# A fused attention and gated FFN on one Trainium2 core: an attention window of 128 + 104 keys, transposes and PV placed one step later from step 20, and the last output tile in two halves

## The chip, the core and the metric

The kernel runs on one core of one Trainium2 chip. The metric is the device time of one execution, in microseconds. Of before there are three timed runs and one profiled execution.

## The reference

Two stages, all in float32. First an attention with a narrow mask; its output, heads side by side, is then the input of a gated FFN with a convolution over the sequence.

```python
B, H, S, D = 4, 8, 768, 64            # d_model 512, d_ff 1024
n_global, n_local = 8, 96
scores = q @ k.T / sqrt(D)
rel = pos[:, None] - pos[None, :]
keep = (pos[None, :] < n_global) | ((rel >= 0) & (rel < n_local))
dist = where(is_global & ~is_local, n_local, abs(rel))
scores = where(keep, scores - slope[h] * dist, -1e9)
a = exp(scores - max); a = a / (sum(a) + 1e-9)
x = a @ v                              # heads side by side: (B, S, 512)

h = maximum(x @ w_in, 0)
c = conv_w[0]*h[t-1] + conv_w[1]*h[t] + conv_w[2]*h[t+1]
out = (h * sigmoid(c)) @ w_out
```

## The kernel before

**Attention steps.** A sequence has two halves (`u` = 0, 1) of 384 positions (`TB`), a half has three blocks of 128 queries, and heads go in four pairs. A *job* `m` is one batch, one half and one head pair: 32 jobs, in the order batch, half, pair, so that four jobs with `u` = 0 alternate with four with `u` = 1. A *step* `s` is one block of a job: 96 steps, three to a job. A block of queries sees 232 keys (`WIN`): the 96 before it, its own 128, and the 8 global ones. These lie in two chunks: the 128 keys from 96 before the block up to its 32nd own key, then the 8 global keys with the other 96 own keys (104). The first block of a sequence (`first`: `u` = 0, block 0) has no keys before it: it works on 136 keys, of which 32 lie in the first chunk and 104 in the second. There are 16 such blocks, one in each job with `u` = 0.

A step is: `scores` (TensorE matmuls per head: one in plain float32 in the first nine jobs, L359; later two in float32r, L369), `maxima` (VectorE adds the bias table and takes the minimum, L386), `exps` (ScalarE, into one of three buffers `pbuf`, L398), `normalise` (reciprocal on VectorE, L410; the scaling on GpSimd, L416, and up to step 39 for the second head on ScalarE, L414), `transposes` (four on TensorE, L424 and L425, to PSUM, and a copy to `pt` by ScalarE, L431, or in two parts for a first block, L428 and L429). When the three blocks of a job are there, `values` does PV: for each block and chunk one float32 matmul per head, the two heads side by side in the array's columns (L447). In the trace a plain float32 PV matmul is two records. `mixed` then splits the result into two float32r parts, `xh` and `xl` (L459, L460).

**FFN.** For each half `n`: eight groups `h` of 12 matmuls of 384 columns (L478, `relu` into `hbuf` L488), the convolution (L524 GpSimd, L525 and L526 VectorE), tanh (L544), a test that its values are not saturated (`sat`, L555), the gate and its split (L577 to L580), and output tiles `o` of 128 rows by 512 columns, 24 matmuls each (L589), copied (L603) and stored. Its matmuls are the fill: they are put in portions between the attention work of the steps (`fill`).

**What sets the order.** Up to step 10 (`HAND` = 11) the order on every engine is that of the code. After that a scheduler places what the loop hands it; the loop issues in step `s` the scores, maxima and exps of `s`, the normalisation of `s` − 1, the transposes of `s` − 2 (`LAG_T`) and, where a job ends there, the PV of step `s` − 4 (`LAG_V`). The fill is spread by `e = s - LAG_V - 1`: the FFN of a half joins the queue when its last job has been mixed. SyncE issues nearly all loads in one queue, among them `v` (L113, two buffers, so the load of a job waits for the PV of the job before the last), `rk` (L104) and `rq` (L105), which GpSimd casts (L125, L131).

**The end.** Each engine's program holds a second, general path (`general`), which runs if the inputs do not suit the fast one. From step 96 on the weights' words are loaded once more and tested in 16 pieces (`check_load` L314, `check_piece` L321 on VectorE and L325 on ScalarE). After the last output tile, whose two column halves ScalarE (L597) and VectorE (L599) copy and two queues store (L600, L601), the matmul `total` (L832) and one comparison (L833) make a flag; every engine reads it (L936) and branches over `general` (L937). L944 is the closing barrier.

## Time and profile before

| | |
|---|---|
| timed runs | 464.76, 466.29, 466.71 us; median 466.29 |
| profiled execution | 466.18 us |
| its span, first to last instruction | 464.2 us |
| TensorE matmul busy | 443.3 us, 96% of the span |
| VectorE, ScalarE, GpSimd busy | 354.5, 304.4, 223.0 us |
| DMA | 60.01 MB, mean 129 GB/s |

The profiled execution takes 2.0 us more than its span, which lies before the first and after the last recorded instruction. Ends of matmuls are modelled, so a busy TensorE says that it had work, not that it was at its peak; what a matmul costs in a stream is read from the distance between starts.

### The profile page before, as it was taken

What the parts mean: (1) busy time and instruction counts of PE and PEld (TensorE: products, weight loads), DVE (VectorE), ACT (ScalarE), POOL (GpSimd) and SP (SyncE); (2) the same over time, 40 slices, a digit from 0 to 9 for tenths busy, and PEclk for the clock granted to TensorE, in tenths of its full rate; (3) what the DMA queues carried; (4) which work ended last, traced back from release to release, by engine and by line L of the source; (5) the groups of instructions that cost most, each with busy time, mean ns of one, the idle gap of its engine ahead of it and who ended that gap; (6) DMA issues with size and microseconds to landing.
All of it is one profiled execution on the core that took longest, in us unless ns stands there. A gap on an engine that the chain in (4) does not pass through costs nothing.

```text
span 464.2 us, 9113 instructions
## 1 busy us (share of the span) xinstructions
PE 443.3 (96%) x3078; PEld 382.3 (82%) x3078; DVE 354.5 (76%) x928; ACT 304.4 (66%) x854; POOL 223.0 (48%) x311
## 2 busy tenths in 40 slices
PE   8978999889979999999999999999999999998994
PEld 7756788679868998888978988889988988897883
DVE  6877999979988978677889987847989877358600
ACT  3757778679689586556667587647776595557510
POOL 4542555643833783265666785646675451013000
PEclk9999999999999999999999999999999999999998
DMA  8979952333334413433334323442334233672111
GB/s 223 244 201 228 277 164 72 104 106 114 114 114 117 145 39 125 122 122 112 114 114 157 105 85 105 117 138 80 110 122 150 80 89 109 260 259 92 45 45 52
DMA packets 21221, 60.01 MB, mean 129 GB/s; under 512 B 2736, under 2 KB 2992, under 8 KB 21168
## 3 DMA queue, kind: packets, MB, share of 16 engines
q1 hardware_dynamic: 17488, 53.01, 37.5%
q10 hardware_dynamic: 3680, 6.36, 3.7%
q8 instruction: 26, 0.43, 0.4%
q14 instruction: 27, 0.22, 0.2%
HBM read 53.07 MB, written 6.29 MB: 128 GB/s over the span
## 4 chain that ended last, share of the span: by engine, by line
PE 64%; DMA 3%; DVE 1%; ACT 1%; issue 1%; ACTq 0%; DVEq 0%; SPq 0%
PE o L589 26%; PE h L478 19%; PE pv L447 7%; PE s L369 6%; PE t L424 3%; DMA check<-in_w 3%; PE t L425 3%; ACT junkb L325 0%; DVE c L525 0%; DVE junk L321 0%; DVE c L526 0%; ACT sat L555 0%; DVE oc L599 0%; ACT ob L597 0%; ACT hbuf L488 0%
## 5 line engine op out<-in xcount | busy, mean ns | idle before, releaser
L416 POOL TENSOR_SCALAR pbuf<-pbuf,mm 128x232 f32<-128x232 f32 (+1 forms) x152 | 108.4, 723 | 91.1 <-DVE mm L410 58.2
L398 ACT ACTIVATE pbuf<-s,mm 128x232 f32<-128x232 f32 (+1 forms) x192 | 83.8, 443 | 51.6 <-DVE mm L386 30.6
L386 DVE CUSTOM_DVE_ANT_0 s<-s,tab 128x232 f32<-128x232 f32 (+1 forms) x192 | 73.5, 385 | 32.8 <-PE s L369 22.4
L524 POOL TENSOR_SCALAR c<-hbuf,cw 128x382 f32<-128x382 f32 (+1 forms) x64 | 49.7, 780 | 58.9 <-ACT hbuf L488 53.8
L589 PE MATMUL o<-woh,gh 128*128 128x512 f32 x192 | 77.2, 402 | 0.0
L589 PE MATMUL o<-wol,gh 128*128 128x512 f32 x192 | 76.5, 398 | 0.0
L589 PE MATMUL o<-woh,gl 128*128 128x512 f32 x192 | 76.1, 397 | 0.0
L478 PE MATMUL h<-xh,wih 128*128 128x384 f32 x252 | 58.7, 345 | 1.4 <-ACT hbuf L488 1.4
L478 PE MATMUL h<-xl,wih 128*128 128x384 f32 x252 | 59.2, 343 | 0.0
L478 PE MATMUL h<-xh,wil 128*128 128x384 f32 x252 | 57.0, 342 | 0.0
L431 ACT ACTIVATE pt<-t 128x512 f32<-128x512 f32 x80 | 48.1, 605 | 13.2 <-PE t L425 12.3
L447 PE MATMUL pv<-pt,v 104*64 104x128 f32 (+2 forms) x768 | 54.0, 280 | 2.3 <-ACT pt L431 1.6
L424 PE MATMUL t<-ident,pbuf 128*128 128x128 f32 (+1 forms) x192 | 49.5, 279 | 5.7 <-issue 2.0
L447 PEld LDWEIGHTS pv<-pt,v 104*64 104x64 f32 (+2 forms) x768 | 40.7, 135 | 16.1 <-issue 7.9
L425 PE MATMUL t<-ident,pbuf 128*128 128x128 f32 x192 | 48.6, 274 | 0.0
L525 DVE SCALAR_TENSOR_TENSOR c<-hbuf,cw,c 128x382 f32<-128x382 f32 (+1 forms) x64 | 44.0, 698 | 3.1 <-POOL c L524 2.8
L478 PEld LDWEIGHTS h<-xh,wih 128*128 128x128 f32 x252 | 43.0, 189 | 3.9 <-ACT hbuf L488 1.7
L526 DVE SCALAR_TENSOR_TENSOR c<-hbuf,cw,c 128x382 f32<-128x382 f32 (+1 forms) x64 | 44.5, 702 | 0.4
L478 PEld LDWEIGHTS h<-xh,wil 128*128 128x128 f32 x252 | 43.8, 188 | 1.2 <-issue 1.1
L478 PEld LDWEIGHTS h<-xl,wih 128*128 128x128 f32 x252 | 43.9, 188 | 0.8 <-issue 0.8
L589 PEld LDWEIGHTS o<-woh,gl 128*128 128x128 f32 x192 | 36.1, 188 | 8.2 <-issue 0.2
L488 ACT ACTIVATE hbuf<-h 128x384 f32<-128x384 f32 x64 | 31.7, 501 | 16.1 <-PE h L478 15.4
(109 smaller groups left out, 866.6 us busy)
## 6 DMA issues: line engine op xcount, KB each, us to landing
v<-in_vv SPq DMA_DIRECT2D x32, 384.0 KB, 3.4
rq<-in_qk SPq DMA_DIRECT2D x23, 384.0 KB, 3.1
wr<-in_w SPq DMA_DIRECT2D x16, 512.0 KB, 5.7
check<-in_w SPq DMA_DIRECT2D x16, 512.0 KB, 4.5
rk<-in_qk SPq DMA_DIRECT2D x12, 504.0 KB, 3.8
out<-ob ACTq DMA_DIRECT2D x23, 256.0 KB, 2.0
rk<-in_qk SPq DMA_DIRECT2D x11, 408.0 KB, 3.6
rq<-in_qk SPq DMA_DIRECT2D x8, 192.0 KB, 6.0
```

The lines of the kernel that those rows point to most:

```text
L386: last_ttr[s] = V.tensor_tensor_reduce(out=sp[j][:, c0 : c0 + n], in0=sp[j][:, c0 : c0 + n], in1=tb, scale=-0.125, scalar=3.0e38, op0=ALU. ...
L398: last_exp[s] = A.activation(pb[:, j, c0 : c0 + n], sp[j][:, c0 : c0 + n], AF.Exp, bias=mm[:, j : j + 1], scale=-1.0, accum_out=mm[:, 2 + ...
L416: G.tensor_scalar(x, x, inv, 1.0, ALU.mult, ALU.mult)
L424: T.transpose(pt[:ka, j, 0, :], pb[:, j, c0:P], ident)
L425: T.transpose(pt[:, j, 1, :], pb[:, j, P:256], ident)
L431: last_ev[s] = A.activation(sb, pt, AF.Copy)
L447: T.matmul(pv[m][64 * j : 64 * j + 64, i * P : (i + 1) * P], vt[m][:n, i, c, 64 * j : 64 * j + 64], sb[:n, j, c, :], start=c == 0, stop=c ...
L478: T.matmul(ps[:, :TB], w_[:, k, fs], x_, start=part == 0 and k == 0, stop=part == 2 and k == NK - 1,)
L524: G.tensor_scalar(c, *tap(1), 1.0, ALU.mult, ALU.mult)
L525: V.scalar_tensor_tensor(c, *tap(0), c, ALU.mult, ALU.add)
L526: V.scalar_tensor_tensor(c, *tap(2), c, ALU.mult, ALU.add)
L589: T.matmul(ps, g_[:, f], w_[:, f], start=f == 0 and part == 0, stop=f == NF - 1 and part == 2,)
```

## The change

**Keys.** The second chunk now holds 104 own keys (from the 24th own key on, `NEAR` = 24), and the 8 global keys stand at the end of the first chunk, behind 96 earlier keys and 24 own ones. The 104 own keys are not visible to the block's first 24 queries, so the PV matmul of that chunk takes 104 query columns instead of 128. A first block is 128 keys in one chunk (`W0` = 128): one transpose per head instead of two, one copy, and one PV matmul per head instead of two. The two heads of a step lie side by side in `pbuf` (232 columns each), so head 0's second chunk is transposed together with head 1's first 24 columns; those rows are not used. `pt` holds chunks ahead of heads.

**Lags.** From step 20 (`LONGER`) transposes come 3 steps behind and PV 5 steps behind; step 20 itself issues neither, and the loop runs one step longer at the end. There are four `pbuf`.

**End.** The tests' last part and the flag (`verdict`) stand ahead of the last output tile. That tile is made in two halves of 256 columns, each copied by ScalarE and stored from its queue. Branch hints for `general` are put on TensorE and VectorE behind the flag and on ScalarE at step 48 (`HINT`).

```diff
-W0 = P + NGLOB
+W0 = P
+NEAR = P - NPREV - NGLOB
+NLATE = P - NEAR
-LAG_T, LAG_V = 2, 4
-NPB = 3
+LAGS, LONGER = ((2, 4), (3, 5)), 20
+NPB, NPT = 4, 4
+HINT = 48
...
-        cols += glob + list(range(q0 + 32, q0 + P + (32 if i < NB - 1 else 0)))
+        cols += list(range(NGLOB))
+        cols += list(range(q0 + NEAR, q0 + P + (NEAR if i < NB - 1 else 0)))
...
-    pbuf = [const.tile([P, 2, 256], F32, name=f"pbuf{i}") for i in range(NPB)]
+    pbuf = [const.tile([P, WIN + 256], F32, name=f"pbuf{i}") for i in range(NPB)]
...
     def transposes(s):
         m, i = steps[s]
-        pb, c0, _, _ = st_s.pop(s)
+        pb, n, _ = st_s.pop(s)
         pt = ps_t.tile([P, 2, 2, P], F32, tag="t", name=f"t{s}")
-        ka = P - c0
         for j in range(2):
-            T.transpose(pt[:ka, j, 0, :], pb[:, j, c0:P], ident)
-            T.transpose(pt[:, j, 1, :], pb[:, j, P:256], ident)
-        sb = p2.tile([P, 2, 2, P], F32, tag="pt", name=f"pt{s}", bufs=NB + 1)
-        if c0:
-            A.activation(sb[:ka, :, 0], pt[:ka, :, 0], AF.Copy)
-            A.activation(sb[:, :, 1], pt[:, :, 1], AF.Copy)
-        else:
-            last_ev[s] = A.activation(sb, pt, AF.Copy)
-        st_pt[s] = (sb, ka)
+            T.transpose(pt[:, 0, j], pb[:, j * WIN : j * WIN + P], ident)
+            if n > P:
+                T.transpose(pt[:, 1, j], pb[:, j * WIN + P : j * WIN + 256], ident)
+        sb = p2.tile([P, 2, 2, P], F32, tag="pt", name=f"pt{s}", bufs=NPT)
+        k = 2 if n > P else 1
+        last_ev[s] = A.activation(sb[:, :k], pt[:, :k], AF.Copy)
+        st_pt[s] = sb
...
     def block(m, i):
-        sb, ka = st_pt.pop(NB * m + i)
-        for c, n in ((0, ka), (1, P - 24)):
+        sb = st_pt.pop(NB * m + i)
+        whole = jobs[m][1] == 0 and i == 0
+        for c, n, q in ((0, P, 0),) if whole else ((0, P, 0), (1, NLATE, NEAR)):
             for j in range(2):
                 T.matmul(
-                    pv[m][64 * j : 64 * j + 64, i * P : (i + 1) * P],
+                    pv[m][64 * j : 64 * j + 64, i * P + q : (i + 1) * P],
                     vt[m][:n, i, c, 64 * j : 64 * j + 64],
-                    sb[:n, j, c, :],
+                    sb[:n, c, j, q:],
                     start=c == 0,
-                    stop=c == 1,
+                    stop=c == 1 or whole,
                 )
...
-    hand = True
-    for s in range(len(steps) + LAG_V + 1):
+    hand, out_of = True, -1
+    for s in range(len(steps) + LAGS[1][1] + 1):
         cur["s"] = s
+        lag_t, lag_v = cur["lags"] = LAGS[s >= LONGER]
...
-            e = s - LAG_V - 1
+            e = s - lag_v - 1
+            fresh, out_of = e != out_of, e
...
-            if ends(s - LAG_V):
-                values((s - LAG_V) // NB)
-            if s < len(steps) + LAG_T:
-                transposes(s - LAG_T)
+            if ends(s - lag_v) and s != LONGER:
+                values((s - lag_v) // NB)
+            if s < len(steps) + lag_t and s != LONGER:
+                transposes(s - lag_t)
...
+        if s == HINT:
+            with tc.issue_after(last_exp[s].ins):
+                tc.mark_branch_hint_location(
+                    "general", "LikelyTaken", [mybir.EngineType.Activation]
+                )
...
+    def last_tiles(ahead=None):
+        for b, t in tiles_of(NU - 1)[:-1]:
             for f in range(NF):
                 mm2(b, t, f)
+        if ahead:
+            ahead()
+        b, t = tiles_of(NU - 1)[-1]
+        gh, gl = gt[b, t]
+        o = p1.tile([P, NF, S - CB], F32, tag="c", name=f"oc{b}_{t}")
+        x = DM // 2
+        for k in range(2):
+            ps = ps_m.tile([P, 512], F32, tag="m", name=f"o{b}_{t}_{k}")
+            c = slice(k * x, (k + 1) * x)
+            for f in range(NF):
+                for part, (g_, w_) in enumerate(((gh, woh), (gh, wol), (gl, woh))):
+                    T.matmul(
+                        ps[:, :x], g_[:, f], w_[:, f, c],
+                        start=f == 0 and part == 0, stop=f == NF - 1 and part == 2,
+                    )
+            A.activation(o[:, k, :x], ps[:, :x], AF.Copy)
+            nc.scalar.dma_start(out[b, t * P : (t + 1) * P, c], o[:, k, :x])
+
+    def verdict():
+        check_weights()
+        check_gates()
+        total = ps_v.tile([P, 512], F32, tag="v", name="total")
+        E = mybir.EngineType
+        at = (
+            (E.PE, T.matmul(total[0:1, 0:1], bad, ones, start=True, stop=True)),
+            (E.DVE, V.tensor_scalar(flag[0:1], total[0:1, 0:1], 0.5, None, ALU.is_gt)),
+        )
+        for engine, last in at:
+            with tc.issue_after(last.ins):
+                tc.mark_branch_hint_location("general", "LikelyTaken", [engine])
-    last_tiles()
+    last_tiles(verdict)
```

How the order moves, in three places. The first is TensorE's PV group of a job with `u` = 0 in the middle of the program (job 16; `pv` is its result, `pt` the three transposed blocks, `v` its values; the shape is that of the output of one head). Before:

```order
L478 MATMUL h_1_2736<-xl_2520,wih 128x384
L478 MATMUL h_1_2736<-xl_2663,wih 128x384
L447 MATMUL pv_2768<-pt_2681,v_2507 64x128 x4
L447 MATMUL pv_2768<-pt_2580,v_2507 64x128 x4
L447 MATMUL pv_2768<-pt_2636,v_2507 64x128 x4
L478 MATMUL h_1_2736<-xh_2181,wil 128x384
```

After:

```order
L477 MATMUL h_0_2686<-xh_2502,wil 128x384
L446 MATMUL pv_2742<-pt_2661,v_2425 64x128 x2
L446 MATMUL pv_2742<-pt_2661,v_2425 64x104 x2
L446 MATMUL pv_2742<-pt_2553,v_2425 64x128 x2
L446 MATMUL pv_2742<-pt_2613,v_2425 64x128 x2
L446 MATMUL pv_2742<-pt_2613,v_2425 64x104 x2
L477 MATMUL h_0_2686<-xh_2642,wil 128x384
```

Twelve matmuls of 128 columns have become six of 128 and four of 104; the first block, the middle row, has one chunk left.

The second place is the end of the fast path on TensorE (`o` is an output tile, `misc` holds the tests' results). Before:

```order
L589 MATMUL o_5_5516<-woh,gh_5_5427 128x512
L589 MATMUL o_5_5516<-wol,gh_5_5427 128x512
L589 MATMUL o_5_5516<-woh,gl_5_5428 128x512
L832 MATMUL total<-misc 1x1
L936 TENSOR_LOAD misc
L937 COMPARE_AND_BRANCH
```

After (between the first and the last of these rows stand 48 matmuls of 256 columns in all):

```order
L588 MATMUL o_4_5409<-woh,gl_4_5329 128x512
L848 MATMUL total<-misc 1x1
L967 BRANCH_PREFETCH_HINT
L835 MATMUL o_5_0_5452<-woh,gh_5_5348 128x256
L835 MATMUL o_5_0_5452<-wol,gh_5_5348 128x256
...
L835 MATMUL o_5_1_5479<-wol,gh_5_5348 128x256
L835 MATMUL o_5_1_5479<-woh,gl_5_5349 128x256
L959 TENSOR_LOAD misc
L960 COMPARE_AND_BRANCH
```

The flag's matmul has moved ahead of the last tile, and the branch now follows the tile's last matmul.

The third place is VectorE in the last FFN half, where the tests of the weights' words (`junk<-check`) meet the convolution (`c<-hbuf,cw,c`). Before:

```order
L525 SCALAR_TENSOR_TENSOR c_5190<-hbuf,cw,c_5190 128x386 x2
L526 SCALAR_TENSOR_TENSOR c_5190<-hbuf,cw,c_5190 128x386 x2
L321 ISA junk_5277,misc<-check_5208 128x512
L321 ISA misc 128x1
L525 SCALAR_TENSOR_TENSOR c_5190<-hbuf,cw,c_5190 128x386
L321 ISA junk_5302,misc<-check_5232 128x512
L321 ISA misc 128x1
L526 SCALAR_TENSOR_TENSOR c_5190<-hbuf,cw,c_5190 128x386
L321 ISA junk_5326,misc<-check_5257 128x512
```

After:

```order
L322 ISA junk_5222,misc<-check_5153 128x512
L322 ISA misc 128x1
L524 SCALAR_TENSOR_TENSOR c_5117<-hbuf,cw,c_5117 128x386
L525 SCALAR_TENSOR_TENSOR c_5117<-hbuf,cw,c_5117 128x386
L524 SCALAR_TENSOR_TENSOR c_5117<-hbuf,cw,c_5117 128x386
L322 ISA junk_5245,misc<-check_5177 128x512
L322 ISA misc 128x1
L525 SCALAR_TENSOR_TENSOR c_5117<-hbuf,cw,c_5117 128x386
L322 ISA junk_5267,misc<-check_5202 128x512
L322 ISA misc 128x1
L524 SCALAR_TENSOR_TENSOR c_5117<-hbuf,cw,c_5117 128x386
```

Before, five of the 16 test pieces stand behind the first taps of this convolution; now two do.

## Rows read from the trace of the kernel before

**Rows 1.** The page's first part: the span, and busy time, share of the span and number of records of each engine.

```profile
span 464.2 us, 9113 instructions
PE 443.3 (96%) x3078; PEld 382.3 (82%) x3078; DVE 354.5 (76%) x928; ACT 304.4 (66%) x854; POOL 223.0 (48%) x311
```

**Rows 2.** Four stretches of the span: length, busy time of PE, PEld, DVE, ACT and POOL with the number of records, granted clock, DMA share and GB/s.

```profile
68.00:100.00 32.00, 28.11 (x204) 23.26 (x203) 29.42 (x80) 25.02 (x81) 18.25 (x24) 1.00 0.33 98
100.00:140.00 40.00, 37.09 (x268) 32.50 (x267) 35.34 (x79) 32.11 (x96) 21.84 (x24) 1.00 0.34 113
140.00:395.00 255.00, 255.00 (x1788) 224.90 (x1787) 206.20 (x531) 173.24 (x469) 144.94 (x192) 1.00 0.35 113
395.00:421.00 26.00, 24.57 (x145) 22.16 (x144) 12.87 (x30) 16.41 (x40) 3.17 (x5) 1.00 0.73 255
```

**Rows 3.** What TensorE waited for between 68 and 140 us: total us, times, longest.

```profile
PE s L369 <- ACT pbuf L398: 2.3, 2, 1.4
PE t L424 <- issue: 2.0, 2, 1.5
PE pv L447 <- ACT pt L431: 1.6, 1, 1.6
```

**Rows 4.** Two stretches, PV's instructions alone (busy time and records of PE, PEld, DVE and ACT that write or read `pv`).

```profile
60.00:140.00 80.00, 11.53 (x168) 8.81 (x168) 3.85 (x7) 3.42 (x7) 1.00 0.35 109
140.00:395.00 255.00, 33.43 (x480) 25.51 (x480) 11.02 (x20) 10.04 (x20) 1.00 0.35 113
```

**Rows 5.** Two PV groups in the chain of work, one of a job with `u` = 1 and one of a job with `u` = 0: start, length in us.

```profile
297.44 1.47 PE pv L447 x24
...
308.99 1.76 PE pv L447 x24
```

**Rows 6.** TensorE's weight loads of one PV group with `u` = 0 (first three rows) and one with `u` = 1: start, length, rows*columns of the weights, count, and in brackets the idle time before.

```profile
208.60 0.42 PEld L447 LDWEIGHTS pv<-pt,v 128*64 128x64 f32 x8 [0.25 <-issue]
209.19 0.19 PEld L447 LDWEIGHTS pv<-pt,v 32*64 32x64 f32 x4 [0.17 <-issue]
209.55 0.64 PEld L447 LDWEIGHTS pv<-pt,v 104*64 104x64 f32 x12 [0.17 <-issue]
...
254.09 1.30 PEld L447 LDWEIGHTS pv<-pt,v 128*64 128x64 f32 x24 [0.25 <-issue]
```

**Rows 7.** Two scores of the first nine jobs, four records each, of 232 and of 136 columns in plain float32: start, length.

```profile
26.69 1.05 PE L359 MATMUL s<-rk,rq 64*128 64x232 f32 x4
...
30.09 0.73 PE L359 MATMUL s<-rk,rq 64*128 64x136 f32 x4
```

**Rows 8.** Starts on TensorE in a dense stretch: transposes and scores of a first block, then scores of 232 columns.

```profile
196.10 0.27 PE L424 MATMUL t<-ident,pbuf 128*32 128x128 f32 x1
196.21 0.27 PE L425 MATMUL t<-ident,pbuf 128*128 128x128 f32 x1
...
196.50 0.27 PE L369 MATMUL s<-kk,qh 128*128 128x136 f32 x1
196.60 0.28 PE L369 MATMUL s<-kk,ql 128*128 128x136 f32 x1
...
302.62 0.28 PE L369 MATMUL s<-kk,ql 128*128 128x232 f32 x1
302.73 0.27 PE L369 MATMUL s<-kk,qh 128*128 128x232 f32 x1
```

**Rows 9.** The end of the chain of work: a load of the tests, the wait before the last matmul groups, and these.

```profile
407.73 5.13 DMA check<-in_w
...
418.06 0.92 ACT sat L555 x2
418.98 0.38 ACT hbuf L488
...
419.40 4.43 PE h L478 x24
423.84 33.61 PE o L589 x144
```

**Rows 10.** The issue of the last two stores: start, length.

```profile
457.88 0.34 ACTq L600 DMA_DIRECT2D out<-ob  x1
...
458.66 0.35 SPq L601 DMA_DIRECT2D out<-oc  x1
```

**Rows 11.** The same two stores among the DMA issues: count, KB, us from issue to landing.

```profile
out<-ob ACTq DMA_DIRECT2D x1, 128.0 KB, 1.7
out<-oc SPq DMA_DIRECT2D x1, 128.0 KB, 3.6
```

**Rows 12.** Line 937, the branch over the general path, and the semaphores waited for behind it: durations in ns (min/median/max), first and last start.

```profile
L937 SPq EVENT_SEMAPHORE  x8: 17/17/17, 459.6 to 462.6; - x8
...
L937 PEldq COMPARE_BRANCH  x1: 4057/4057/4057, 458.4 to 458.4; - x1
...
L937 ACTq COMPARE_BRANCH  x1: 54/54/54, 458.8 to 458.8; - x1
...
L937 ACTq EVENT_SEMAPHORE  x1: 17/17/17, 462.6 to 462.6; - x1
```

**Rows 13.** The load queue's own waits: us in total, times, longest.

```profile
SPq L113 <- PE pv L447: 87.4, 22, 12.1
```

**Rows 14.** Who waited for the loads of line 104 (`rk`), in us and times.

```profile
  POOL kk L125: 3.4, 4
```

## The prediction, written before the changed kernel ran

> **What bounds the kernel now.** I read the busy shares first, then stretches, then TensorE's waits, and last the end of the chain. TensorE is at 96% with VectorE next at 76% [rows 1]. The mean hides four parts [rows 2]. From 140 to 395 us TensorE has work in all of the 255 us, VectorE in 206 of them: here only less TensorE work, or a new wait, moves the time. From 68 to 140 TensorE has work in 65.2 of 72 us while VectorE stands at 29.4 of 32 and 35.3 of 40; TensorE's waits are for ScalarE's exponentials (2.3 us), for transposes whose input is late (2.0) and for a copied transpose ahead of PV (1.6) [rows 3]. Here both engines bind, and a saving on TensorE counts in part. Before that the program follows a written order with warm-up matmuls in it; I give nothing for what TensorE saves there. From 395 to 421 the chain runs through the loads of the tests, and TensorE waits once, until 419.40, for a copy of `h` that stands behind `sat` on ScalarE [rows 9]; it idles 1.4 us in this stretch [rows 2]. The last 144 output matmuls take 33.61 us, 0.233 each [rows 9]. They end near 457.45, and the span at 464.2 [rows 1]: 6.7 us with no matmul but the flag's.

> **PV.** A group takes 1.47 us in a job with `u` = 1 and 1.76 with `u` = 0 [rows 5], with 24 records in both. The loads show why [rows 6]: the ordinary group is one run of 24, the other is cut in three, before and behind the four loads of 32 rows, with 0.17 us idle at each cut. The 32-row chunk costs 1.76 − 1.47 = 0.29 us beyond its records, and the change has no such chunk. It also has one chunk less, four records in two pairs. The 24 loads of the ordinary group take 1.30 us, the last of them about 0.13, so 12 pairs start 1.17/11 = 0.106 us apart; two pairs are 0.21 us. Together 0.50 us per job with `u` = 0.

> The other second chunks go from 128 to 104 columns. No matmul of 104 columns is in the trace. If the loads set the pace the gain is nothing; if the columns do, it follows [rows 7]: four records of 232 columns take 1.05 us, of 136 columns 0.73, and 0.32 us over 96 columns and four records is 0.83 ns per column. A PV pair of 128 columns would by that take 0.107 us, which is what it takes, so I let columns set the pace: 24 columns are 0.020 us for each of two pairs, 0.04 per block, 0.12 per job with `u` = 1 and 0.08 with `u` = 0. The bounds are 0 and this. [...]

> So a job with `u` = 0 saves 0.58 us in PV, one with `u` = 1 0.12. Between 140 and 395 us stand 20 groups (480 records) and between 60 and 140 seven (168) [rows 4]. In the order of jobs, four before 60 us, the seven are four with `u` = 1 and three with `u` = 0, and the 20 are nine with `u` = 0 and eleven with `u` = 1. In the dense stretch PV gives 9 × 0.58 + 11 × 0.12 = 6.5 us.

> **Transposes and scores.** Transposes start 0.11 us apart [rows 8], with two fewer in a first block: 0.22 us. Eight first blocks (jobs 16 to 19 and 24 to 27) are transposed in the dense stretch: 1.8 us. Scores go from 136 to 128 columns there, for nothing, since at 136 columns they start 0.10 to 0.11 us apart, as at 232 [rows 8]. ScalarE's single copy and the shorter exponentials lie on an engine busy 173 of 255 us [rows 2]. Dense stretch together: **8.3 us**, counted whole because no other engine is near its limit.

> From 60 to 140 us: 3 × 0.58 + 4 × 0.12 + 4 × 0.22 = 3.1 us of TensorE work. VectorE is busy nine tenths of the time and keeps its work; bounds 0 and 3.1, and I take half, **1.5**.

> **Lags.** From step 20 a transpose may be a step later than its input, and a step is 255 us over some 58 steps, 4.4 us. That covers the 3.6 us of waits at transposes and PV, not the 2.3 at scores [rows 3]. Some will come back as waits elsewhere, as VectorE is nearly full; bounds 0 and 3.6, I take **1.5**. Against it: all FFN work from step 20 on is issued one step later. If the early stretch stays as long as VectorE makes it, one step's portion of fill moves out of it into the dense one. A portion is some 3 of 40 units (24 thirds of `h` groups' work and 16 of `o`) spread over 13 steps, and a unit of three `o` matmuls is 0.70 us: 2.1 us; bounds 0 and that, I take half, **−1.1**. Both are guesses between ends and nearly cancel.

> **Tail.** After the last scores there is now more fill ahead of the last half's `h` groups, and of the tests on VectorE only two pieces stand among the taps instead of five. Cover for the loads grows, and the wait at 419.40 has less reason. It is worth up to the 1.4 us idle there; I take **1.0**. If the loads still come last, the wait stays, and shorter PV only lengthens it.

> **End.** Last tile: 24 matmuls of 512 columns are 5.6 us. Matmuls of 232 columns start 0.11 apart [rows 8], those of 512 0.233; on the line between them 256 columns are 0.12, and 48 are 5.3 to 5.8 us: nothing either way. The flag is now known before that tile, on VectorE's side while it idles. Before, three things came last within 0.4 us of each other: the store from SyncE, issued at 458.66 [rows 10], landing 3.6 us later [rows 11] at 462.3; TensorE, whose branch at 458.4 took 4057 ns; ScalarE, which branched at 458.8 in 54 ns and then reached its next instruction only at 462.6 [rows 12]. From 462.6 the closing barrier takes 1.6 us. In the change SyncE stores nothing, and TensorE and SyncE have the flag early. The last store stands on ScalarE at what was 457.88, lands 1.7 us later at 459.6, and the same semaphores and barrier behind a landing, 464.2 − 462.3 = 1.9 us, give 461.5: **2.7 us** less, if ScalarE's 3.8 us after the branch are gone too. No hint is in the trace of before, so bounds are 0 and 2.7. I take 2.7, because TensorE and ScalarE are the only ones that stalled past the store, and each has a hint or cover.

> **Sum.** 8.3 + 1.5 + 1.5 − 1.1 + 1.0 + 2.7 = 13.9 us from the profiled execution's 466.2, its span of 464.2 with 2.0 around it: **452.3 us**. The median of the timed runs, 466.29, is the same within 0.1, so nothing is added.

> **Rivals.**

> *ScalarE's hint does nothing.* It is given at step 48 of 96, half of all steps before the branch. Then ScalarE reaches its last semaphore at what was 462.6 [rows 12] and the end is as late as before: 452.3 + 2.7 = 455.0. For it: nothing in the trace shows a hint holding so long. Against it: the stall begins only behind the branch, so anything that names its target earlier can help. [...] Chance 0.2.

> *The step is set by its chain, not by TensorE.* Scores, maxima, exponentials and scaling pass through four engines, and if that loop is nearly as long as TensorE's portion, half of the dense stretch's 8.3 us turns into waits, and the early terms vanish: 466.2 − 4.2 − 2.7 = 459.3. For it: VectorE at 81% there with long instructions in order, and GpSimd at 57% [rows 2]. Against it: not a microsecond of idle TensorE in 255. Chance 0.13.

> *Slower: loads.* SyncE's queue is in order, and the load of `v` waits for PV two jobs back: 22 waits, 87.4 us [rows 13]. That PV is now a step, 4.4 us, later; behind it stand `rk` and `rq`, and GpSimd already waited 3.4 us in four casts for `rk` [rows 14]. GpSimd scales the probabilities in the same order, so a late cast delays transposes. If each of the 19 later jobs lost 1 us of TensorE, the sum would be 452.3 + 19 = 471.3; from 0.73 us per job on the kernel is no faster. Against it: the casts are issued two to three steps before the scores that read them, 9 to 13 us, and transposes have a step more room. Chance 0.04.

> *The parts cancel*, 464 to 468.5: 0.03, for the terms are independent.

> **Numbers.** The sum as it stands has 0.6, with its own range of 447 to 456: 0 for the columns and the lags' gain at one end; at the other the early stretch whole, 3.6 for waits, and nothing lost in fill, another 5 us. The first two rivals lie at 455 and 459.3. A range of 447 to 459.5 leaves out less than the slow cases and half of the second rival. The three runs lie 0.4% apart; I call 0.5%, 2.3 us, what can be told from no change. Faster by more than that: 0.6 + 0.2 + 0.13, less a little for mistakes in my reading, 0.91; same 0.05; slower 0.04.

> **What the profile after would show.** Right: PV groups of 20 records in about 1.18 us and of 24 in 1.35, one unbroken run of loads; TensorE still without idle time in the dense stretch, which ends 8 us sooner; no wait behind `sat` near the end; every engine past its branch before the last store lands, and 4.0 us from last matmul to end instead of 6.7. Wrong: PV pairs of 104 columns still 0.106 us apart; waits of TensorE for `pbuf` or `pt` after step 20, or of GpSimd for `rk`; 3.8 us behind ScalarE's branch. I am most likely wrong about the half terms between 60 and 140 us and about the hint.

## The result, and the profile after

After takes 453.59 us (median of 4, from 453.08 to 454.38), before 466.33 beside it: ratio 0.973, 95% interval 0.971 to 0.976. 452.3 was predicted, with a range of 447.0 to 459.5. Medians, ratios and intervals leave out the slow executions, those over 1.5% above the fastest of their kernel: at most two in a set, one of them of 1397.68 us with more warm-up.

The first part of the page after, which answers to [rows 1]:

```profile
span 451.9 us, 8953 instructions
PE 431.7 (96%) x3006; PEld 377.6 (84%) x3006; DVE 356.2 (79%) x927; ACT 302.0 (67%) x839; POOL 229.4 (51%) x310
```

TensorE is still the bound, with 11.6 us less busy time. To see where the 12.3 us of the span came from, both executions are cut at the same points of the program instead of the same times: where VectorE begins the maxima of the steps 20, 39 and 95, and at the last matmul (the flag's left out). Before, then after; the columns are those of [rows 2]:

```profile
0.00:68.70 68.70, 62.71 (x521) 50.20 (x522) 56.06 (x180) 44.38 (x147) 32.33 (x66) 0.98 0.81 222
68.70:141.90 73.20, 66.40 (x477) 56.96 (x478) 64.76 (x161) 58.33 (x181) 41.60 (x49) 1.00 0.32 102
141.90:381.30 239.40, 239.40 (x1698) 212.22 (x1697) 196.25 (x507) 163.36 (x447) 141.45 (x185) 1.00 0.36 113
381.30:457.50 76.20, 74.77 (x386) 62.88 (x385) 36.90 (x79) 37.96 (x83) 7.59 (x12) 1.00 0.37 128
```

```profile
0.00:69.80 69.80, 62.07 (x497) 49.60 (x497) 54.76 (x180) 43.33 (x142) 32.67 (x66) 0.95 0.79 222
69.80:140.20 70.40, 62.93 (x452) 54.49 (x453) 65.34 (x161) 58.59 (x176) 41.32 (x47) 1.00 0.33 102
140.20:370.50 230.30, 230.28 (x1639) 208.00 (x1638) 197.06 (x508) 160.47 (x440) 146.56 (x185) 1.00 0.38 118
370.50:447.90 77.40, 76.42 (x422) 65.53 (x420) 39.02 (x81) 39.18 (x82) 8.86 (x13) 1.00 0.38 128
```

The stretches changed by +1.1, −2.8, −9.1 and +1.2 us, and behind the last matmul 6.7 us became 4.0. The length minus TensorE's busy time is its idle time: between the steps 20 and 39 it did not shrink (6.8 before, 7.5 after), so there are not fewer waits there in sum. Behind step 95 there are 36 records more. 24 of them are no added work: the last tile is now 48 matmuls of 256 columns instead of 24 of 512. Counted by their starts, four transposes and seven output matmuls, some 2.1 us, have moved there: four of the seven from the steps 20 to 39, the other three and the transposes from the steps 39 to 95.

Two PV groups in the chain of work of after, as in [rows 5] (start, length):

```profile
153.89 1.35 PE pv L446 x24
...
205.04 1.17 PE pv L446 x20
```

Before they were 1.47 and 1.76 us. All 21 groups behind 135 us have one of these two lengths, before as after. PV alone between the steps 39 and 95, in the columns of [rows 4], before and after:

```profile
141.90:381.30 239.40, 31.89 (x456) 24.21 (x456) 10.48 (x19) 9.55 (x19) 1.00 0.36 113
...
140.20:370.50 230.30, 25.35 (x420) 21.52 (x420) 10.40 (x19) 9.51 (x19) 1.00 0.38 118
```

It takes 6.5 us less. Near the end the chain of after still has a load of the tests and `sat`, as in [rows 9], and then one unbroken run of output matmuls:

```profile
396.76 6.94 DMA check<-in_w
...
412.96 1.03 ACT sat L554 x2
413.99 0.38 ACT hbuf L487
...
414.42 27.75 PE o L588 x120
442.17 0.12 PE total L848 x2
442.29 5.66 PE o L835 x48
```

The branch over `general`, as in [rows 12]:

```profile
L960 DVEq COMPARE_BRANCH  x1: 84/84/84, 443.1 to 443.1; - x1
...
L960 PEldq COMPARE_BRANCH  x1: 390/390/390, 446.3 to 446.3; - x1
L960 DVEq EVENT_SEMAPHORE  x1: 21/21/21, 446.5 to 446.5; - x1
...
L960 ACTq COMPARE_BRANCH  x1: 76/76/76, 449.3 to 449.3; - x1
L960 ACTq EVENT_SEMAPHORE  x1: 17/17/17, 449.8 to 449.8; - x1
```

ScalarE reaches its next instruction 0.5 us behind the start of its branch instead of 3.8, and TensorE's branch takes 0.39 us instead of 4.06. VectorE still stands for 3.4 us behind its branch, which costs nothing: it is through at 446.5, before the last matmul ends at 447.9.

### The profile page after: what moved, and what is told of

It is laid out like the page before. It is cut to its first block, busy times and chain, and to the rows that moved or that the text cites. A ratio compares the mean times of both kernels' runs of the same rounds, so it can differ in the third digit from the quotient of the medians.

```text
span 451.9 us, 8953 instructions
## 1 busy us (share of the span) xinstructions
PE 431.7 (96%) x3006; PEld 377.6 (84%) x3006; DVE 356.2 (79%) x927; ACT 302.0 (67%) x839; POOL 229.4 (51%) x310
## 4 chain that ended last, share of the span: by engine, by line
PE 76%; DVE 13%; DMA 4%; ACT 3%; issue 2%; POOL 1%; DVEq 0%; ACTq 0%; SPq 0%; POOLq 0%
PE o L588 24%; PE h L477 24%; PE pv L446 8%; PE s L370 7%; PE t L424 4%; DMA check<-in_w 4%; PE s L360 3%; PE t L426 3%; DVE s L387 3%; DVE c L525 2%; DVE c L524 2%; PE o L835 1%; ACT pbuf L399 1%; DVE junk L322 1%; DVE w L296 1%
## 5 line engine op out<-in xcount | busy, mean ns | idle before, releaser
L588 PE MATMUL o<-woh,gh 128*128 128x512 f32 x184 | 74.9, 407 | 0.1
L588 PE MATMUL o<-wol,gh 128*128 128x512 f32 x184 | 72.6, 395 | 0.0
L588 PE MATMUL o<-woh,gl 128*128 128x512 f32 x184 | 72.5, 395 | 0.0
L429 ACT ACTIVATE pt<-t 128x512 f32<-128x512 f32 (+1 forms) x96 | 54.0, 564 | 14.9 <-PE t L426 11.5
L477 PE MATMUL h<-xl,wih 128*128 128x384 f32 x252 | 57.4, 342 | 0.0
L424 PE MATMUL t<-ident,pbuf 128*128 128x128 f32 x192 | 48.2, 280 | 6.1 <-POOL pbuf L417 2.6
L524 DVE SCALAR_TENSOR_TENSOR c<-hbuf,cw,c 128x382 f32<-128x382 f32 (+1 forms) x64 | 46.3, 731 | 9.3 <-POOL c L523 9.2
L525 DVE SCALAR_TENSOR_TENSOR c<-hbuf,cw,c 128x382 f32<-128x382 f32 (+1 forms) x64 | 45.3, 713 | 0.5
L446 PEld LDWEIGHTS pv<-pt,v 128*64 128x64 f32 (+1 forms) x704 | 36.1, 136 | 8.7 <-issue 2.9
L446 PE MATMUL pv<-pt,v 128*64 128x128 f32 (+1 forms) x704 | 42.6, 268 | 0.7 <-DVE xl L459 0.7
L543 ACT ACTIVATE c<-c 128x764 f32<-128x764 f32 (+1 forms) x32 | 27.1, 848 | 21.6 <-DVE c L525 21.5
L426 PE MATMUL t<-ident,pbuf 128*128 128x128 f32 x160 | 39.7, 276 | 0.6 <-ACT pbuf L415 0.5
```

The lines of the kernel that those rows point to most:

```text
L424: T.transpose(pt[:, 0, j], pb[:, j * WIN : j * WIN + P], ident)
L426: T.transpose(pt[:, 1, j], pb[:, j * WIN + P : j * WIN + 256], ident)
L429: last_ev[s] = A.activation(sb[:, :k], pt[:, :k], AF.Copy)
L446: T.matmul(pv[m][64 * j : 64 * j + 64, i * P + q : (i + 1) * P], vt[m][:n, i, c, 64 * j : 64 * j + 64], sb[:n, c, j, q:], start=c == 0, st ...
L477: T.matmul(ps[:, :TB], w_[:, k, fs], x_, start=part == 0 and k == 0, stop=part == 2 and k == NK - 1,)
L524: V.scalar_tensor_tensor(c, *tap(0), c, ALU.mult, ALU.add)
```

## The experiments

Each kernel was timed against before on its own chip. The table gives the lengths of the stretches above in each profile, with TensorE's idle time in brackets (length minus busy time); the last column is from the last matmul to the end. Along a row one sees where a kernel gains, and from row to row what brings the gain. The medians and the lengths to step 20 go with the granted clock (68.6 us at 0.98 in one profile, 73.0 at 0.88 in another; below). Between the steps 20 and 39 the clock is 1.00 but for 0.98 with three `pbuf`, PV on 128 columns, lags from step 40 and more warm-up, and 0.95 with the lags alone; between 39 and the last matmul it is 1.00 in all. Each row is one profiled execution: the two of after differ by 1.2 us from step 20 to the end.

| kernel | median us | to step 20 | 20 to 39 | 39 to 95 | 95 to last matmul | behind |
|---|---|---|---|---|---|---|
| before | 466.3 | 68.7 | 73.2 (6.8) | 239.4 (0) | 76.2 (1.4) | 6.7 |
| before, heads side by side, three `pbuf` | 465.8 | 68.3 | 76.0 (6.8) | 238.8 (0) | 75.6 (1.2) | 6.7 |
| before, side by side, four `pbuf` | 465.8 | 72.4 | 70.0 (4.1) | 240.2 (0.4) | 74.9 (0.6) | 6.4 |
| the same with the longer lags | 471.0 | 73.8 | 71.8 (4.0) | 238.5 (0.1) | 77.5 (0.3) | 6.7 |
| keys and four `pbuf` alone | 458.7 | 68.6 | 69.2 (4.9) | 236.5 (4.0) | 74.6 (0.7) | 6.4 |
| after without longer lags | 457.1 | 69.7 | 69.1 (5.0) | 237.1 (4.5) | 74.0 (0.2) | 4.0 |
| after | 453.6 | 69.8 | 70.4 (7.5) | 230.3 (0) | 77.4 (1.0) | 4.0 |
| after again | 457.4 | 73.0 | 70.1 (7.4) | 230.3 (0) | 76.5 (0) | 4.0 |
| after, PV on 128 columns | 455.5 | 68.8 | 70.8 (5.2) | 232.0 (1.1) | 77.7 (0.9) | 4.0 |
| after, longer lags from step 40 | 455.7 | 72.5 | 69.7 (3.9) | 231.7 (2.5) | 76.4 (0) | 4.0 |
| after, more warm-up | 451.6 | 66.7 | 72.2 (6.9) | 229.4 (0) | 76.3 (0) | 4.0 |

### The parts alone

**Keys alone**: `LAGS, LONGER = ((2, 4), (2, 4)), 10**6` in after, and the end of before.

> The new key layout and the one-chunk first blocks alone (with four pbuf), lags of 2 and 4 throughout and the end of before. The prediction's terms: 8.3 us in the dense stretch and 1.5 between 60 and 140 us, 466.3 - 9.8 = 456.5. A rival that gives the lags more (two thirds of what after gained between steps 20 and 95 needs them): about 460. A rival in which the tail takes it back, because shorter PV only brings the wait for the test loads forward (1.0 us of it kept): 457.5.

458.70 us, ratio 0.985 (0.980 to 0.990): between the prediction's 456.5 and the 460 of the rival. The reason stands in the table: TensorE idles 4.0 us between the steps 39 and 95, where before had none, and that stretch became 2.9 us shorter where the prices of the prediction give 8.2 for its 19 groups.

**Lags alone**: `LAGS, LONGER, NPB = ((2, 4), (3, 5)), 20, 4` and the loop of after in before, with `pbuf` of `WIN + 256` columns as in after; what that shape and the fourth buffer do without the lags was run by itself (below).

> Before, with the longer lags from step 20 alone (four pbuf, the two heads side by side in them; keys, chunks and end as before). The prediction's terms: 1.5 less waiting, 1.1 lost in fill, 1.0 gained at the loads of the tests: 466.3 - 1.4 = 464.9. Rival, from the trace of after, whose TensorE idles as long between steps 20 and 39 as before's (7.5 us against 6.8) and whose stretch behind step 95 is 1.2 us longer: the lags move one portion of fill and take no wait away, 466.3 or at most 0.3 less. Rival, the gain of after from step 20 on needs the lags: 463 or less.

470.98 us, ratio 1.012 (1.008 to 1.016): no theory had this. The loss lies ahead of step 20, where the lags are the old ones: 73.8 us at a mean granted clock of 0.91, against 68.7 at 0.98. The clock is 0.95 between the steps 20 and 39 too. Why all six executions had a lower mean clock than before (0.970 to 0.979) stays open. Against the run with four buffers and no lags (below), the dense stretch, from step 39 to 95, is 1.7 us shorter and the one behind step 95 2.6 longer. Ten output matmuls (2.3 us) have moved over step 95, seven from the steps 20 to 39 and three from the dense stretch. With the old keys there was next to no idle time in the dense stretch for the lags to take away (0.4 us, 0.1 with them).

**End alone**: before with `last_tiles(verdict)` and the three hints.

> Before, with the shorter end alone (flag ahead of the last tile, two halves, the three hints). The prediction: from the last matmul to the end 4.0 us instead of 6.7, and nothing in the tail: 466.3 - 2.7 = 463.6. Rival, the hint on ScalarE helps only where the rest of the program is shorter, or not at all: 466.3. Rival, the end adds to its gain by taking the flag's operations out of the path: 463.0 or less.

463.44 us, ratio 0.994 (0.992 to 0.996), 2.55 less in the medians; 4.2 us from the last matmul to the end instead of 6.7. The prediction's 463.6.

**After without the longer lags.**

```diff
-LAGS, LONGER = ((2, 4), (3, 5)), 20
+LAGS, LONGER = ((2, 4), (2, 4)), 10**6
```

> After, with lags of 2 and 4 throughout. The prediction's terms: 1.5 of waits come back, 1.1 of fill is regained and 1.0 at the loads of the tests is lost: 453.6 + 1.4 = 455.0. Rival, the lags only move a portion of fill: 453.6, with step 20 to 39 longer and the stretch behind step 95 shorter by the same 1 to 2 us. Rival, they hide waits that the new layout makes (two heads side by side, one step's transposes waiting for both): 457 or more.

457.05 us, ratio 0.982 (0.977 to 0.987); from step 20 to the end 384.2 us against 382.1 in after, all at a clock of 1.00. So the lags are worth 2.1 us in equal stretches (3.3 against the second profile of after), with a gain where none was expected: 6.8 us between the steps 39 and 95, of which 4.5 are idle time, against losses of 1.3 and 3.4 around it. Of the rest of the 6.8, 0.9 is work that moved behind step 95: four transposes and two output matmuls, beside five output matmuls from the steps 20 to 39. What TensorE waited for between 138 and 376 us (total us, times, longest):

```profile
PE pv L446 <- issue: 2.4, 1, 2.4
PE t L426 <- ACT pbuf L415: 0.8, 1, 0.8
PE h L477 <- ACT xh L458: 0.7, 1, 0.7
PE t L424 <- POOL pbuf L417: 0.4, 1, 0.4
```

The first has no releaser by the profile. It ends at 252.13 us, and VectorE's instructions up to then are (start, length):

```profile
248.50 1.21 DVE L579 TENSOR_TENSOR gl<-c,gh 128x1024 fp32r<-128x1024 f32 x1
249.64 0.40 DVE L387 CUSTOM_DVE_ANT_0 s<-s,tab 128x232 f32<-128x232 f32 x1
...
249.96 1.22 DVE L579 TENSOR_TENSOR gl<-c,gh 128x1024 fp32r<-128x1024 f32 x1
...
251.49 0.54 DVE L459 TENSOR_TENSOR xl<-pv,xh 128x384 fp32r<-128x384 f32 x1
```

There is one PSUM buffer for `pv`. The PV matmuls start 0.10 us behind the end of `xl` (252.03), which reads the PV result before it and stood behind two splits of the gate. TensorE's queue had stood at a semaphore since 247.5 us:

```profile
L446 PEldq EVENT_SEMAPHORE  x2: 51/2324/4596, 240.4 to 247.5; - x2
```

The other inputs were there by then: the last copy to `pt` ends at 248.30, and the load of `v`, issued at 244.75, lands at most 3.7 us later. With the keys alone the like wait, 1.8 us, ends 0.11 us behind `xl`. All this fits a wait for that buffer; a second buffer was not tried.

### PV's columns

```diff
-        for c, n, q in ((0, P, 0),) if whole else ((0, P, 0), (1, NLATE, NEAR)):
+        for c, n, q in ((0, P, 0),) if whole else ((0, P, 0), (1, NLATE, 0)):
```

> After, with the second chunk's PV matmuls on all 128 query columns again (the first 24 columns add zeros). If the columns set the pace, as the prediction took it, a PV group is 0.12 us longer with u = 1 and 0.08 with u = 0: 16 x 0.20 = 3.2 us in the whole program, 2.0 of them between 140 and 395 us, so 455.6 to 456.8 against 453.6 for after, with groups of 24 records in 1.47 us. If the weight loads set it (the rival), groups stay at 1.35 us and the time at 453.6.

Its PV groups in the chain:

```profile
151.15 1.47 PE pv L446 x24
...
205.14 1.25 PE pv L446 x20
```

The groups are 0.12 and 0.08 us longer with the same number of weight loads, so in these groups the columns set the pace: a pair of 104 columns takes 0.020 us less than one of 128. PV alone between the steps 39 and 95, at a clock of 1.00 in both runs, takes 1.92 us more than the 25.35 of after:

```profile
139.60:371.60 232.00, 27.27 (x420) 22.68 (x420) 10.46 (x19) 9.51 (x19) 1.00 0.37 117
```

That is 9 × 0.08 + 10 × 0.12 us, just what the columns give. The whole from step 20 to 95, 302.8 us against 300.7, is no such measure: the clock is 0.98 up to step 39, and the fill is spread differently. Nor is the median, 455.47 (ratio 0.982, 0.977 to 0.987): the expectation was 455.6 to 456.8, but the two sets of after, below, lie at 453.59 and 457.44.

### Hints

ScalarE's hint left out (the block `if s == HINT`), then all three.

> After, without ScalarE's branch hint at step 48; TensorE's and VectorE's stay. If that hint is what lets ScalarE through (the prediction), its next instruction comes 3.8 us behind its branch at 449.3, at 453.1, and the end 1.6 us later: 454.7 instead of 451.9, so 456.4 in time. The rival, that the hint at step 48 is too early to do anything and something else shortened the end: 453.6.

> After, without any of the three hints. The prediction's step: TensorE has the flag early, reaches its branch at 447.9 with its last matmul and stalls 4.1 us to 452.0, VectorE's stall lies earlier, so both stay behind ScalarE's 453.1: 456.4, no more than without ScalarE's hint alone. Rival, TensorE's stall behind its own last matmul sets the end: 457.5 or more. Rival, no hint does anything: 453.6.

The medians, 456.24 and 454.47 us (ratios 0.982 and 0.975, both ± 0.005), stand in the wrong order and can't tell a microsecond; the ends of the traces can. Without ScalarE's hint:

```profile
L955 ACTq COMPARE_BRANCH  x1: 54/54/54, 448.7 to 448.7; - x1
L955 ACTq EVENT_SEMAPHORE  x1: 17/17/17, 451.4 to 451.4; - x1
```

Without any (an execution at a mean granted clock of 0.97):

```profile
L952 PEldq COMPARE_BRANCH  x1: 3634/3634/3634, 450.7 to 450.7; - x1
L952 ACTq COMPARE_BRANCH  x1: 54/54/54, 453.7 to 453.7; - x1
L952 PEldq EVENT_SEMAPHORE  x1: 51/51/51, 454.4 to 454.4; - x1
L952 ACTq EVENT_SEMAPHORE  x1: 17/17/17, 456.2 to 456.2; - x1
```

ScalarE stalls 2.7 and 2.5 us from its branch on, against 0.5 with the hint given at 184.7 us, 265 us earlier: given so early, it still went with a stall 2.2 us shorter. But of the 2.2 us only 1.0 sets the end (5.0 us behind the last matmul instead of 4.0; 4.8 without any hint), because the last store lands meanwhile: in after it lands at 450.13 us, 0.3 us behind ScalarE's next instruction, and the closing barrier follows it; without the hint it lands at 449.55 and ScalarE comes at 451.4. TensorE's stall of 3.63 us begins ahead of its last matmul's end and is over before ScalarE's: its hint gives nothing here. VectorE's hint comes 0.8 us ahead of its branch in after, and VectorE stalls 3.4 us with it and 3.3 without; whether a hint further ahead would help it was not tried. The other 1.8 of the 2.7 us come with the rest of the new end (the flag ahead of the last tile, one queue, a half-size last store), which was not taken apart further. Why ScalarE's stall was 3.8 us in before and 2.7 here was not tried.

### Lags from step 40

```diff
-LAGS, LONGER = ((2, 4), (3, 5)), 20
+LAGS, LONGER = ((2, 4), (3, 5)), 40
```

> After, with the longer lags from step 40 on instead of 20. From the runs so far: in the steps 20 to 39 TensorE idles 5.0 us with lags of 2 and 4 and 7.5 with 3 and 5, behind step 39 4.4 against 0. If the two stretches add, the steps 20 to 39 take 69.1 instead of 70.4 us and the rest stays: 452.3. Rival, the waits at the steps 40 to 42 (2 us) stay because the change of lags comes too late for them: 454.5. Rival, only the number of steps matters by which fill is late: 453.6.

455.73 us, ratio 0.975 (0.971 to 0.979). From step 20 to the end 381.8 us against 382.1: no gain that can be told. Half of the early idle time is gone (3.9 instead of 7.5) and 2.5 us of idle come back behind step 39, so the second part of the sum did not hold. The first can't be judged to a microsecond: the clock is 0.98 there against 1.00, and the stretch holds five output matmuls (1.2 us) that after has later.

### The clock

**After again**, unchanged, then **before with four `pbuf`** side by side and no longer lags (what the lags alone had beside them).

> After once more, unchanged, beside the two runs below. If its times hang only on its work, 453.6 again. If the clock that TensorE is granted in the first 70 us decides the spread (the variants of after so far lie between 451.1 us at a mean clock of 1.00 and 459 at 0.97), single runs should spread over 451 to 459 and line up with their clock, and the profile should show the first 70 us at another clock than the 0.50 to 0.67 between 12 and 20 us of the first profile of after.

> Before, with four pbuf and the two heads side by side in them, but lags of 2 and 4 throughout: what the run with the lags alone had beside its lags. That run lost 5.1 us ahead of step 20, where its lags are still those of before, with TensorE's clock at half from 44 to 54 us. If the buffers' layout brings that, this run takes 470 to 471 and shows the same clock. If it does not, 466.3, and the lags alone are then judged from step 20 on, where that run was 1.0 us shorter than before. Rival, the layout costs waits and not clock: longer idle time of TensorE ahead of step 20.

After again: 457.44 us, ratio 0.982 (0.977 to 0.987), against 453.59 for the same kernel earlier. Single runs went from 453.28 us at a mean granted clock of 0.992 to 463.48 at 0.959. From step 20 to the end its profile is 380.9 us, after's first 382.1; the difference lies ahead of it. In after, two stretches (the third column from the right is the clock):

```profile
0.00:11.60 11.60, 9.37 (x94) 8.29 (x94) 6.99 (x30) 3.96 (x12) 5.31 (x28) 1.00 0.80 219
11.60:20.00 8.40, 8.40 (x58) 7.30 (x59) 3.83 (x14) 4.20 (x15) 2.89 (x3) 0.59 0.77 233
```

In after again the clock falls elsewhere:

```profile
0.00:32.00 32.00, 27.07 (x274) 21.98 (x274) 22.86 (x83) 17.07 (x57) 15.33 (x43) 1.00 0.85 237
32.00:52.00 20.00, 18.19 (x83) 13.53 (x84) 14.09 (x45) 11.69 (x41) 7.40 (x10) 0.57 0.59 165
```

Ahead of both falls TensorE waited at transposes, 1.2 us in two waits between 10 and 12 and 2.2 us up to 33.7 (in after 36.5). Not each such wait was followed by a fall: in after the second one was not (a clock of 1.00 from 20 us on), in after again the first (1.00 up to 32 us). Of the profiles with the keys of after, four show the fall at the second wait: their mean clock between 32 and 36 us is 0.82 (the keys alone), 0.83 (PV on 128 columns), 0.89 (without hints) and 0.84 (after again). After and after without longer lags have 0.98 and 0.94 between 8 and 12 us instead, 0.50 from 12 to 16 us, and 1.00 between 32 and 36. In before, where the second wait is 1.5 us, the clock falls there too (0.70 between 32 and 36 us); with the end alone, where TensorE has work in as little of these four microseconds (2.53), it is 1.00.

Before with four buffers: 465.78 us, ratio 0.999 (0.996 to 1.002). It is not slower, so the buffers alone do not bring the 471. But it hides a gain: from step 20 on 391.6 us against 395.5 in before, lost again ahead of step 20 at a clock of 0.93.

**More warm-up**: after with

```diff
             if s >= lag_t:
+                warm({2: 10, 9: 36}.get(s, 0))
                 transposes(s - lag_t)
```

> After, with 10 more warm-up matmuls ahead of the transposes of step 2 and 36 ahead of those of step 9, where TensorE waits 1.2 and 2.2 us in after; they are no part of the result. If waits in the written order are what lets the clock fall, the clock stays near 1.00 there, step 20 comes at 67.5 to 68.5 us instead of 69.8 and the time is 451 to 452.5. If the extra matmuls only push the scores behind them back, step 20 comes later by up to their 2.4 us: 454 to 456. If the fall of the clock has nothing to do with these waits: 453.6.

451.63 us, ratio 0.970 (0.966 to 0.974), the fastest kernel here: beside it on the same chip after had 457.44. The stretch in which after again lost its clock:

```profile
32.00:52.00 20.00, 18.49 (x161) 14.40 (x158) 18.76 (x61) 15.71 (x53) 9.54 (x13) 1.00 0.87 240
```

Step 20 comes at 66.7 us instead of 69.8 and 73.0. The mean clock of its five executions is 0.983 to 1.000, that of after again's six 0.959 to 0.992. That fits the theory that these waits let the clock fall, and shows no more of it. What makes a wait do so in one execution and not in another stays open.

### Which part of `pbuf`

Before with the heads side by side and three buffers.

> Before, with the two heads side by side in pbuf but three of them as before. With four (the run before this one), the steps 20 to 39 took 70.0 us instead of 73.2, and ScalarE's 5.6 us of waits for the transposes that free a pbuf were gone. If the fourth buffer does that, this run has 73 us in the steps 20 to 39, ScalarE's waits of 5 to 6 us for transposes again, and before's time at an equal clock. If the side-by-side layout does it, 70 us and no such waits.

465.83 us, ratio 1.000 (0.998 to 1.003). Its steps 20 to 39 took 76.0 us, partly at a lower clock (0.98) and with six output matmuls (1.4 us) more, and with the idle time of before, 6.8. The four buffers have 4.1 and 70.0 us. In before, ScalarE's exponentials waited between 68.7 and 141.9 us:

```profile
ACT pbuf L398 <- PE t L425: 5.6, 4, 2.5
```

With four buffers no such wait is among its largest seven. With three and the new layout it is 1.0 us, less than expected, and other waits are longer:

```profile
ACT c L545 <- DVE c L527: 4.1, 4, 1.1
...
ACT pbuf L399 <- PE t L426: 1.0, 2, 0.7
```

By the stretch and by TensorE's idle time it is the fourth buffer, not its layout, that shortens these steps; by ScalarE's row alone it could not be told.

## Why the prediction was right, and where it was not

**PV and transposes: right.** 1.18 and 1.35 us were predicted for the groups, 1.17 and 1.35 came. The column count, the doubtful term, is real: a pair of 104 columns takes 0.020 us less than one of 128. TensorE had work in all of the dense stretch again, which became 9.1 us shorter. The prediction's 8.3 are for 140 to 395 us; for the 19 groups between the steps 39 and 95 its prices give 8.2, and four transposes and three output matmuls that moved behind step 95 give 1.1. But less work alone did not bring this: without the longer lags, 4.5 us of it came back as waits.

**60 to 140 us: about the right sum, wrong parts.** 1.5 for keys, 1.5 for lags and −1.1 for moved fill were predicted; 2.8 came between the steps 20 and 39. By single profiles, the fourth `pbuf` gave 3.2, the keys 0.8 beyond it, and the lags took 1.3, though they moved five output matmuls (1.2 us) out of this stretch. That the sum is near is luck. The step that failed is the one that read TensorE's waits alone: the row of ScalarE above, in the trace of before, names the buffer, and the prediction gave it no term.

**Lags: wrong mechanism, sum near.** +1.5 and −1.1 were predicted, 2.1 to 3.3 measured with the new keys. They did not take away the waits of [rows 3]: of the 3.6 us at transposes and PV the fourth buffer alone left 1.2, and with the lags TensorE's waits for `pbuf` at scores between the steps 20 and 39 are 5.2 us, against 2.6 without them: a sign of being wrong that the prediction had named. With the old keys they gave nothing. They remove waits that arise in the dense stretch only once TensorE has less to do there (4.5 us). That is the second rival in part: some half of what the keys gained turned into waits, and the lags, which this rival left out, got it back. The moved fill was taken for a loss of the dense stretch; against after without the longer lags it is seven output matmuls (1.6 us) that came to the tail, five of them from the steps 20 to 39 and two from the dense stretch, so that stretch got none.

**Tail: uncertain.** 1.0 was predicted; TensorE's idle time there fell from 1.4 to 1.0 us in the first profile and to 0 in the second. In the second the wait behind `sat` is gone. In the first the loads of the tests are still in the chain and the wait for `hbuf` is left (behind step 95: total us, times, longest):

```profile
PE h L477 <- ACT hbuf L487: 0.9, 1, 0.9
```

The stretch itself became 1.2 and 0.3 us longer, since moved work came to it.

**End: right, its condition wrong.** 2.7 predicted, 2.7 measured. The first rival said that without ScalarE's hint all of it is lost; it is 1.0 us. The step took the stall of before, 3.8 us, as given.

**Loads: did not come.** SyncE's wait for PV, 87.4 us in [rows 13], fell, and its wait for VectorE's `ql`, which reads the `rq` loaded before, grew from 61.3 us:

```profile
SPq L108 <- DVE ql L135: 94.2, 14, 10.9
...
SPq L116 <- PE pv L446: 37.7, 14, 11.0
```

So much of the queue's wait only changed its place: over the loads of `v`, `rk` and `rq` it is 266 us instead of 290. GpSimd waited longer for `rk`, 5.6 us instead of 3.4 [rows 14], without TensorE losing anything in the dense stretch.

**The first 68 us: left out.** The prediction gave nothing for them. They cost 1.1 us in the first profile and 4.3 in the second. The keys alone, with the same work there, reached step 20 at 68.6 us at a clock of 0.98, after at 69.8 at 0.95 and after again at 73.0 at 0.88, so most of the loss goes with the clock. From step 20 on after gained 13.4 and 14.6 us in its two profiles, on either side of the sum's 13.9. That the first median came within 1.3 us of 452.3 is luck in part: the later set of after, 457.44 us, is 2 us below the upper end of the range, and one of its six executions, 463.48, lies outside.

## What to carry to other kernels

Cut both traces at points of the program, not of time, and look at idle time per stretch: a part of the sum can come out right for another reason, as the early term did here. Before a wait of the bound engine is priced, read the waits of the engines that feed it; a buffer that came free late showed up in them here (5.6 us of ScalarE for `pbuf`). And when work is taken from the bound engine, the next waits can appear where it had none (here 4.5 us without the longer lags), so a change in order can be worth its cost only together with the saving.
